# A planner that keeps VectorE's SBUF steps apart from GpSimd's, with new step times and new weights, in a kernel of attention, a mixture of experts and a SoLU layer

## The chip, the cores and the metric

The kernel runs on one core of a Trainium2 chip as one program. The metric is the device time of that program in microseconds (us). The engines are named as in the profile: PE is TensorE's matmul and PEld its weight load, DVE is VectorE, ACT is ScalarE, POOL is GpSimd, SP is SyncE, which here only starts DMAs. In the kernel's own tables GpSimd is called "Pool".

## The reference

Three layers follow one another, all in float32:

```python
# attention: batch 4, heads 12, sequence 448, head size 64
q_n, k_n = rmsnorm(q, g_q), rmsnorm(k, g_k)
scores = q_n @ k_n.T / sqrt(64);  scores -= max(scores, -1)
attn = exp(scores);  attn /= sum(attn, -1) + 1e-9
x = (attn @ v)                    # -> 1792 tokens x 768
# mixture of 8 experts, each token goes to the argmax of x @ w_gate
out[mask] = gate_w * (relu(x[mask] @ w1[e]) @ w2[e])       # 768 -> 1024 -> 768
# SoLU layer: h = x @ w_in; solu = h * softmax(h); layer norm; @ w_out  (768 -> 1024 -> 768)
```

## The kernel before

**Three stages run one after the other.** First attention with the routing of the tokens (about 0 to 323 us of the trace), then the experts, then the SoLU layer with the scattered stores of the output. The change touches the first stage only; the experts and the SoLU layer are written out by hand in a fixed order.

**Attention works on pairs of heads.** There are 24 pairs, in 9 groups of one to three pairs (`GROUPS`). A pair goes through these steps, each a "task" given to the planner with the time it is thought to take:

- *Group steps* (`group`): DMA loads of q, k and v; ScalarE squares q and k (L311, tile `sq`); for some pairs GpSimd adds the two halves of each head's squares (`half`, L315) so that VectorE's sum (L321) reads half as much; then twelve small VectorE steps, the `chain` (L338 to L347), turn the sums into 1/rms (tile `y`). `half=(0, 1, 1)` in the weights says that the second and third pair of each group from the third group on use GpSimd's addition.
- *Norm and turn* (`pair`): GpSimd multiplies q and k by 1/rms (L423, tile `X`, two steps a pair), PE transposes the result into PSUM (L435), ScalarE writes a rounded "high" half (L458, tile `QQ`), VectorE the remainder as "low" (L461, tile `Q`). SP's DMAs then move half tiles between partitions (L468: `QQ<-QQ`, `KS<-Q`, `K<-KS`), so that one product of 128 rows can hold high and low parts.
- *Row maxima*: seven products of 128 queries by 448 keys (L497, tile `r`), each followed by a VectorE maximum (L508, tile `mx`). PE turns the seven maxima (L520), and a DMA puts them into a row of the operand (`Q<-mr`).
- *Scores and exponentials*: seven blocks (`cut` is their order). PE makes the scores (L497, tile `st`), ScalarE the exponentials (L551, tile `pf`), then `part_h` casts them to float16 (L555, tile `ph`) and `part_l` subtracts to get the float16 remainder (L558, tile `pl`).
- *Values*: PE multiplies `ph` and `pl` with the two halves of v (L587 to L589), which ScalarE and VectorE made (L410 and L413, tile `va`), and VectorE divides (L603, L614, L608).
- *Routing*: after each pair PE turns the output and adds to the logits (L728, L739); after each batch of six pairs some twenty VectorE steps (L782 to L860) choose experts and build the token lists (`ohr`, L809, four steps a batch). After the third batch the `order` steps rank the experts by size, and the first six weight tiles of the largest expert are loaded and the first three split (`w_first`, L1109 and L1114). After the fourth batch comes the table of tokens, and GpSimd's gather of the first expert's tokens (L1129, tile `gx`) starts the second stage.

**The order of all this comes from a planner that runs when the program is built** (`Work.run`). It keeps a clock for each engine. In each round it works out, for every task whose inputs are planned, when it could start: when its inputs are done (plus the table `LAT`), when its engine is free, and when the buffer it takes is free (`ring_time`). Of the tasks that could start within `SLACK` of the earliest it takes the one with the smallest weight (`prio`), and emits its instructions. Each engine then executes its instructions in that order on the chip; the planner's times themselves do not exist there, only the order, the choice of buffers, and the choice of engine. A task whose `eng` is a table of several engines goes to the engine on which the planner's clock sees it finish first. `eh` and `el` hold such tables for `part_h` and `part_l` of the seven blocks; `eh2` and `el2` are for the last pair. `PRIO` holds the weights; a task's weight is its pair's number plus the entry.

Before the change the planner treats VectorE and GpSimd as independent engines.

Of the kernel before, what the change touches and what calls it, by code (L numbers as in the profile page):

```python
# [30 lines left out]
class Work:  # L31
# [13 lines left out]
    SEM = 0.0  # L45
    SLACK = 0.02

    def __init__(self, rings):
        self.tasks = []
        self.rings = rings  # L50
        self.users = {}
        self.light = set()
        self.bufs = {}
        self.place = {}
# [4 lines left out]
    def add(self, eng, dur, fn, deps=(), prio=0.0, take=(), use=(), lat=0.0, dma=0.0):  # L59
# [25 lines left out]
    def run(self):  # L85
        T = self.tasks
        n = len(T)
        left = [len(set(t[2])) for t in T]
        after = [[] for _ in T]
        for i, t in enumerate(T):  # L90
            for d in set(t[2]):
                after[d].append(i)
# [5 lines left out]
        count = 0  # L98
        cols = {}

        def ring_time(i):
            at = dict(ready[i])
            for r, key in T[i][4]:
                q = taken[r]
                if len(q) < self.rings[r]:
                    continue
                free_at = None
                for s in q[:1] if r in self.TURN else q:
                    us = self.users[r, s]
                    if any(end[u] is None for u in us):  # L110
                        continue
                    x = max(end[u] for u in us)
                    if free_at is None or x < free_at[0]:
                        free_at = x, us, s
                if free_at is None:
                    return None
                slot[i, r] = free_at[2]
                for u in free_at[1]:
                    for e in at:
                        at[e] = max(at[e], end[u] + self.LAT[eng_of[u]][e] + self.SEM)  # L120
            return at

        slot = {}
        while cand:
            best = []
            for i in cand:
                rt = ring_time(i)
                if rt is None:
                    continue
                es = []  # L130
                for e, d in T[i][0].items():
                    at = max(rt[e], free.get(e, 0.0))
                    es.append((self.pe_end(cols, at, d, i in self.light) if e == "PE" else at + d, at, e))
                fin, start, e = min(es)
                best.append((start, T[i][3], i, fin, e))
            assert best, "no piece of work can start"
            first = min(best)[0]
            start, prio, i, fin, e = min(
                (b for b in best if b[0] <= first + (self.SLACK0 if first < self.START else self.SLACK)), key=lambda b: (b[1], b[0])
            )  # L140
            for r, key in T[i][4]:
                k = len(taken[r])
                if (i, r) in slot:
                    k = self.place[r, slot[i, r]]
                    taken[r].remove(slot[i, r])
                taken[r].append(key)
                self.place[r, key] = k
            T[i][1](e)
            if e == "PE":
                self.pe_end(cols, start, T[i][0][e], i in self.light, True)  # L150
            end[i], eng_of[i], free[e] = fin + T[i][5], e, fin
            if e == "SP" and T[i][6]:

                free["DMA"] = max(fin + 0.65, free.get("DMA", 0.0)) + T[i][6]
                end[i] = free["DMA"] + T[i][5]
            cand.remove(i)
            count += 1
            for j in after[i]:
                for x in ready[j]:
                    ready[j][x] = max(ready[j][x], end[i] + self.LAT[e][x] + self.SEM)  # L160
# [3 lines left out]
        assert count == n  # L164
# [8 lines left out]
class Attention:  # L173
# [103 lines left out]
    def group(self, g, prio):  # L277
# [27 lines left out]
        for j in range(n):  # L305
            for c in cuts:
# [18 lines left out]
                a = add("ACT", 0.02 + 0.117 * w, squares, [l_kq[j]], prio=p, take=[q], use=[kq, gs])  # L325
                if n_ < D:
                    a = add("Pool", 1.12, half, [a], prio=p + 0.2, use=[q])
                reds.append(add("DVE", 0.08 + 0.155 * w * n_ / D, reduce, [a], prio=p + 0.4, use=[q, gs]))


        def chain(cut, nm, d, prio):
# [17 lines left out]
            for f in steps:  # L349
                a = f is first  # L350
                d = [add("DVE", 0.2, f, d, prio=prio, take=[key] if a else (), use=[gs] + [key] * (not a))]
# [25 lines left out]
        d = add("ACT", 0.2 + 0.37 * n, sumsq, l_v, prio=prio + P["vs"], use=[vv, gs])  # L377
# [13 lines left out]
    def pair(self, m, xt, xkey, last):  # L391
# [23 lines left out]
        d = add("ACT", 0.7, v_high, [self.vs], prio=pv, take=[va_], use=[vk, gs])  # L415
        v_done = self.init3 * (m < 3) + [d, add("DVE", 1.0, v_low, [d], prio=pv, use=[va_, vk, gs])]
# [28 lines left out]
        for w in range(2):  # L445
            i = 2 * m + w
            d_n.append(add("Pool", (1.15, 0.88)[w], lambda e, w=w: norm(e, w), [self.rms[j][w], last.get("norm")], prio=i + P["norm"], take=[X] if w == 0 else [], use=[kq, gs] + [X] * w))
# [24 lines left out]
            for rows, to in cuts:  # L472
                d_h.append(add("ACT", 0.56, lambda e, a=rows, b=to, f=high: f(e, a, b), [d, self.G_done] + d_l, prio=i + P["high"], use=[rT, op]))
                d_l.append(add("DVE", 0.63, lambda e, a=rows, b=to, f=low: f(e, a, b), [d_h[-1]], prio=i + P["low"], use=[rT, op]))
# [36 lines left out]
        for s in range(NS):  # L511
# [4 lines left out]
            d_m.append(add("DVE", 0.57, lambda e, s=s: reduce(e, s), [d0], prio=pr, use=[r, mx]))  # L516
# [21 lines left out]
        d = add({"DVE": 0.18, "ACT": 0.2}, 0, copy_max, [d], prio=pr, take=[mr], use=[r])  # L538
# [24 lines left out]
        for k, s in enumerate(P["cut"]):  # L563
# [7 lines left out]
            d = add(eh[s], 0, lambda e, s=s: part_h(e, s), [d, d_pp] + self.init3 * (m < 2), prio=pr + P["ph"], take=a, use=[pf] + u)  # L571
            if k == 0:
                d_pp = d
            d_p[s] = [d, add(el[s], 0, lambda e, s=s: part_l(e, s), [d], prio=pr + P["pl"], use=[pf, pp])]
# [16 lines left out]
        for w in range(2):  # L591
# [21 lines left out]
            d = add("DVE", 0.19, div1, d, prio=pr, take=[den], use=[gs, av])  # L613
            d = add("DVE", 0.16, lambda e, h=h: V.reciprocal(h["den"], h["den"]), [d], prio=pr, use=[den])  # L614
            last["x"] = add("DVE", 0.4, div3, [d, last.get("x")], prio=pr, take=[xkey] if w == 0 else [], use=[den, av] + [xkey] * w)
# [6 lines left out]
        end=1,  # L622
        half=(0, 1, 1),
        cut=(0, 1, 3, 2, 5, 6, 4),
        cutp=(11.35, 2.17, -0.07, 3.29, -13.81, 10.44, 0.89),
        eh=({'ACT': 0.49, 'DVE': 0.55}, {'ACT': 0.49, 'DVE': 0.55}, {'ACT': 0.49}, {'ACT': 0.49}, {'ACT': 0.49}, {'ACT': 0.49}, {'ACT': 0.49}),
        el=({'Pool': 1.13}, {'Pool': 1.13}, {'Pool': 1.13}, {'DVE': 0.8, 'Pool': 1.13}, {'DVE': 0.8, 'Pool': 1.13}, {'Pool': 1.13}, {'Pool': 1.13}),
# [1226 lines left out]
```

## Time and profile before

| | |
|---|---|
| runs shown | 899.03 us median of 3 (896.51 to 904.44) |
| the profiled execution's own time | 896.94 us |
| its span, first to last instruction | 895.2 us |
| PE busy | 811.1 us (91% of the span) |
| PEld busy | 740.8 us (83%) |
| DVE busy | 641.4 us (72%) |
| ACT busy | 497.8 us (56%) |
| POOL busy | 395.1 us (44%) |

The shares are averages over three stages with different limits; the first stage alone is what the change touches. A row of the list by line reads: line, engine, operation, tile written and tiles read, shapes, how often; then the time its instructions cover in us and the mean of one in ns; then the idle time of the engine just before them and what ended it. The profiled execution is 2.1 us under the median of the runs shown.

### The profile page before, as it was taken

How to read it: one execution, taken by the hardware profiler on the slowest of the kernel's cores; microseconds unless marked ns; L12 is line 12 of the kernel's file. 1: busy time of each engine (PE TensorE's matmuls, PEld its weight loads, DVE VectorE, ACT ScalarE, POOL GpSimd, SP SyncE). 2: the span in 40 equal slices, each digit the busy share in tenths (PEclk: the TensorE clock that was granted, in tenths of full speed). 3: DMA queues.
4: the chain of work that ended last, by engine and by line, in shares of the span. 5: the costliest groups of instructions: out<-in, count | busy, mean ns of one | idle time of the engine just before them, and what ended most of it. 6: DMA issues, size and time to landing. Idle time of an engine off the chain costs nothing.

```text
span 895.2 us, 18893 instructions
## 1 busy us (share of the span) xinstructions
PE 811.1 (91%) x6811; PEld 740.8 (83%) x6811; DVE 641.4 (72%) x1484; ACT 497.8 (56%) x958; POOL 395.1 (44%) x420
## 2 busy tenths in 40 slices
PE   2788998987898959989999999899899999999994
PEld 2577887776787849979999999789779989998994
DVE  7988998897898937998667778788575434444541
ACT  7787988886885805644455556667532323332221
POOL 4777898787784624543674125545110000000000
PEclk9999999999997979999999999999999999999998
DMA  7476575574743355757666777767000000000001
GB/s 207 125 200 171 134 197 145 146 197 83 198 111 83 117 118 164 222 187 244 209 220 202 260 229 250 243 211 245 2 1 36 19 36 19 18 18 36 19 18 38
DMA packets 63871, 120.29 MB, mean 134 GB/s; under 512 B 12159, under 2 KB 35290, under 8 KB 63774
## 3 DMA queue, kind: packets, MB, share of 16 engines
q1 hardware_dynamic: 60478, 107.69, 40.8%
q0 software_dynamic: 3296, 11.35, 4.0%
q8 instruction: 56, 0.92, 0.4%
q14 instruction: 41, 0.34, 0.1%
HBM read 86.08 MB, written 11.03 MB: 108 GB/s over the span
## 4 chain that ended last, share of the span: by engine, by line
PE 36%; issue 26%; DVE 17%; DMA 13%; ACT 4%; POOL 2%; SPq 1%; POOLq 0%; ACTq 0%; DVEq 0%
DMA out_dram<-ot,tok 5%; PE st L497 4%; DMA QQ<-QQ 3%; PE h L1157 3%; DVE mx L508 2%; PE h L1158 2%; PE y L1157 2%; PE h L1159 2%; PE y L1158 2%; PE y L1159 2%; PE r L497 2%; PE h L1154 2%; DMA gx<-xd,gx 2%; PE y L1154 2%; DMA rkq<-in_kq_dram 2%
## 5 line engine op out<-in xcount | busy, mean ns | idle before, releaser
L558 POOL TENSOR_TENSOR pl<-pf,ph 128x448 f16<-128x448 f32 x153 | 166.1, 1105 | 47.7 <-ACT ph L555 16.8
L1359 POOL DMA_INDIRECT out_dram<-ot,tok x14 | 13.8, 987 | 214.3 <-ACT ot L1358 208.8
L508 DVE TENSOR_REDUCE mx<-r 128x1 f32<-128x448 f32 x168 | 99.4, 611 | 12.3 <-PE r L497 11.9
L1114 POOL TENSOR_TENSOR wl<-wr,wh 128x768 fp32r<-128x768 f32 x34 | 64.5, 1899 | 93.6 <-ACT wh L1109 93.1
L1109 ACT CAST wh<-wr 128x768 fp32r<-128x768 f32 x128 | 104.7, 831 | 1.6 <-DMA wr<-in_wmoe_dram 1.6
L1114 DVE TENSOR_TENSOR wl<-wr,wh 128x768 fp32r<-128x768 f32 x94 | 97.5, 1037 | 10.5 <-ACT wh L1109 9.0
L551 ACT ACTIVATE pf<-st 128x448 f32<-128x448 f32 x168 | 86.7, 544 | 22.0 <-PE st L497 19.5
L497 PE MATMUL r<-KS,QQ 128*128 128x448 f32 x192 | 69.0, 428 | 21.0 <-DMA QQ<-QQ 12.1
L555 ACT CAST ph<-pf 128x448 f16<-128x448 f32 x153 | 82.5, 569 | 0.3
L587 PEld LDWEIGHTS <-ph 128*128 128x128 f16 x768 | 71.0, 97 | 12.0 <-issue 10.9
L587 PE MATMUL av<-va,ph 128*128 128x65 f16 x768 | 80.1, 194 | 0.0
L588 PE MATMUL av<-va,ph 128*128 128x64 f16 x768 | 79.7, 195 | 0.0
L589 PE MATMUL av<-va,pl 128*128 128x65 f16 x768 | 79.3, 193 | 0.0
L497 PE MATMUL st<-QQ,KS 128*128 128x448 f32 x192 | 74.4, 408 | 2.7 <-ACT pf L551 2.6
L1320 DVE TENSOR_TENSOR cl<-ct,ch 128x512 fp32r<-128x512 f32 x28 | 18.1, 686 | 80.3 <-ACT ch L1319 80.2
L589 PEld LDWEIGHTS <-pl 128*128 128x128 f16 x768 | 71.6, 99 | 0.0
L588 PEld LDWEIGHTS <-ph 128*128 128x128 f16 x768 | 71.4, 97 | 0.1
L497 PE MATMUL st<-Q,K 128*128 128x448 f32 x192 | 68.7, 378 | 0.5 <-DMA K<-KS 0.5
L1154 PE MATMUL y<-hh,wh 128*128 128x384 f32 (+1 forms) x192 | 61.0, 354 | 7.7 <-DVE hh L1203 7.4
L1154 PE MATMUL h<-xx,wh 128*128 128x384 f32 (+1 forms) x192 | 63.0, 364 | 0.4 <-DVE xx L1184 0.4
L497 PEld LDWEIGHTS r<-KS,QQ 128*128 128x128 f32 x192 | 35.5, 199 | 31.1 <-DVE mx L508 5.9
L1157 PE MATMUL h<-xx,wh 128*128 128x280 f32 (+1 forms) x192 | 57.4, 299 | 0.7 <-DVE hh L1203 0.7
(282 smaller groups left out, 2525.9 us busy)
## 6 DMA issues: line engine op xcount, KB each, us to landing
wr<-in_wmoe_dram SPq DMA_DIRECT2D x128, 384.0 KB
rkq<-in_kq_dram SPq DMA_DIRECT2D x24, 448.0 KB
di<-in_w_in_dram SPq DMA_DIRECT2D x16, 384.0 KB
rv<-in_v_dram SPq DMA_DIRECT2D x24, 256.0 KB
do<-in_w_out_dram SPq DMA_DIRECT2D x16, 384.0 KB
K<-KS SPq DMA_DIRECT2D x48, 112.0 KB
KS<-Q SPq DMA_DIRECT2D x48, 112.0 KB
QQ<-QQ SPq DMA_DIRECT2D x48, 112.0 KB
```

The source lines that it names most:

```text
L497: nc.tensor.matmul(ps[:, :S], H[w][x + "x"][:, columns(w, s)], H[w][y], start=(k == 0), stop=(k == len(n) - 1))
L508: V.tensor_reduce(C["mx"][:, s : s + 1], C["sm", s][:, :S], axis=AX.X, op=ALU.max, negate=True)
L551: nc.scalar.activation(C["pf", s], C["st", s][:, :S], AF.Exp)
L555: (eng[e].copy if e == "ACT" else eng[e].tensor_copy)(ph[s][:, :S], C["pf", s])
L558: eng[e].tensor_tensor(pl[s][:, :S], C["pf", s], ph[s][:, :S], op=ALU.subtract)
L587: nc.tensor.matmul(o, hp, vs[:, 0:65], start=(s == ss[0]), stop=False)
L588: nc.tensor.matmul(o[:, 0:64], hp, vs[:, 65:129], start=False, stop=False)
L589: nc.tensor.matmul(o, lp, vs[:, 0:65], start=False, stop=(s == ss[-1]))
L1109: self.nc.scalar.copy(wh, raw)
L1114: (eng or self.nc.vector).tensor_tensor(wl, raw, f32(wh), op=ALU.subtract)
L1154: mm(ps[:, : 2 * n], wh, xx[:, : 2 * n], start=start, stop=False)
L1157: mm(ps[:, :n], wh, xh, start=start, stop=False)
```

## The change

**The model.** A task may now carry `port=True`; such tasks are kept in a set. All GpSimd tasks, and the VectorE tasks with that mark, are kept apart in the planner's clock: a GpSimd task that would start while a marked VectorE task runs is put at that task's end, and the reverse. Marked are the `chain` steps, `v_low` (L413), `part_h` and `part_l` when on VectorE, and those routing steps that read SBUF only. Not marked are steps with an operand in PSUM and the sums and maxima.

**The step times** of the ScalarE, VectorE and GpSimd tasks are new (for example `chain` steps 0.2 to 0.12 us, `v_low` 1.0 to 0.66, `part_h` on VectorE 0.55 to 0.3 and on ScalarE 0.49 to 0.46, `part_l` on VectorE 0.8 to 0.63 and on GpSimd 1.13 to 1.01).

**The weights** are all new, and with them the order of the blocks, the engine tables and `half`, which is now `(0, 0, 0)`: GpSimd's additions (L315) are gone, and VectorE's sums read the whole of the squares. `part_h` may go to VectorE in five of seven blocks (two before; four of the last pair's, two before), `part_l` in two of seven (two before; three of the last pair's, three before).

**Book-keeping.** `self.lg` becomes a table by batch, `ring_time` keeps results it has worked out, and a task that takes two buffers of one ring is handled. What each task computes is the same.

The core of the diff:

```diff
+    def add(self, eng, dur, fn, deps=(), prio=0.0, take=(), use=(), lat=0.0, dma=0.0, port=False):
+        if port:
+            self.port.add(t)
...
+        pool, dve = (0.0, 0.0), (0.0, 0.0)
...
+                for e, d in t[0].items():
+                    x = max(at[e], free.get(e, 0.0))
+                    if e == "Pool" and dve[0] <= x < dve[1]:
+                        x = dve[1]
+                    elif e == "DVE" and i in port and pool[0] <= x < pool[1]:
+                        x = pool[1]
...
+            elif e == "Pool":
+                pool = start, fin
+            elif e == "DVE" and i in port:
+                dve = start, fin
...
-                    a = add("Pool", 1.12, half, [a], prio=p + 0.2, use=[q])
-                reds.append(add("DVE", 0.08 + 0.155 * w * n_ / D, reduce, [a], prio=p + 0.4, use=[q, gs]))
+                    a = add("Pool", 1.1, half, [a], prio=p + 0.2, use=[q])
+                reds.append(add("DVE", 0.02 + 0.14 * w * n_ / D, reduce, [a], prio=p + 0.4, use=[q, gs]))
...
-        norm=57.16, turn=0.15, high=-61.05, low=-14.42, move=-13.07, movek=15.48, max=2.24, mt=-38.68,
-        scores=23.43, exp=-3.7, ph=-3.92, pl=20.82, values=53.83, div=-34.67, kq=-18.37, v=-13.68, sq=-25.7,
-        rms=-120.46, vs=3.07, vprep=6.16, pair=-36.93, route=8.36, order=46.04, first=34.56, soon=2, nv=2,
-        half=(0, 1, 1),
-        cut=(0, 1, 3, 2, 5, 6, 4),
-        eh=({'ACT': 0.49, 'DVE': 0.55}, {'ACT': 0.49, 'DVE': 0.55}, {'ACT': 0.49}, {'ACT': 0.49}, {'ACT': 0.49}, {'ACT': 0.49}, {'ACT': 0.49}),
-        el=({'Pool': 1.13}, {'Pool': 1.13}, {'Pool': 1.13}, {'DVE': 0.8, 'Pool': 1.13}, {'DVE': 0.8, 'Pool': 1.13}, {'Pool': 1.13}, {'Pool': 1.13}),
+        norm=129.16, turn=-60.25, high=-118.25, low=-108.84, move=8.38, movek=31.93, max=-7.33, mt=-37.11,
+        scores=-9.0, exp=-29.71, ph=-45.83, pl=18.65, values=140.45, div=-29.01, kq=-175.45, v=-3.02,
+        sq=-21.28, rms=-143.95, vs=79.27, vprep=-13.14, pair=-59.93, route=27.67, order=183.91, first=81.87,
+        half=(0, 0, 0),
+        cut=(3, 2, 4, 0, 1, 5, 6),
+        eh=({'ACT': 0.46, 'DVE': 0.3}, {'ACT': 0.46}, {'ACT': 0.46}, {'ACT': 0.46, 'DVE': 0.3}, {'ACT': 0.46, 'DVE': 0.3}, {'ACT': 0.46, 'DVE': 0.3}, {'ACT': 0.46, 'DVE': 0.3}),
+        el=({'Pool': 1.01}, {'Pool': 1.01}, {'Pool': 1.01}, {'Pool': 1.01}, {'DVE': 0.63, 'Pool': 1.01}, {'Pool': 1.01}, {'DVE': 0.63, 'Pool': 1.01}),
```

## Rows read from the trace of the kernel before

**Rows 1.** Three stretches: us, busy us (instructions) of each engine, granted PE clock, DMA share, GB/s.

```profile
0.00:25.00 25.00, 7.84 (x29) 6.28 (x29) 18.96 (x75) 18.37 (x33) 11.12 (x93) 1.00 0.64 187
25.00:325.00 300.00, 267.75 (x3451) 232.02 (x3452) 263.66 (x651) 234.47 (x471) 222.37 (x211) 0.96 0.55 145
325.00:895.00 570.00, 535.53 (x3333) 502.53 (x3332) 358.80 (x759) 244.94 (x456) 161.60 (x118) 0.98 0.40 127
```

**Rows 2.** Waits of PE from 25 to 325 us: us in total, times, longest.

```profile
PE r L497 <- DMA QQ<-QQ: 8.4, 6, 2.3
PE r L497 <- DMA Q<-mr: 3.4, 1, 3.4
PE r L435 <- POOL X L423: 3.1, 1, 3.1
```

**Rows 3.** The chain that ended last, 25 to 325 us, shares by line (cut by the view).

```profile
by line: PE st L497 12.3%; DMA QQ<-QQ 8.6%; DVE mx L508 7.4%; PE r L497 6.7%; issue 6.0%; PE av L587 3.7%; PE av L588 3.6%; PE av L589 3.6%; PE r L435 3.0%; DVE Q L461 3.0%; PE r L739 2.7%; DVE ohr L809 2.6%; DMA KS<-QQ 2.5%; DVE y L347 2.2
```

**Rows 4.** Single lines: shortest/median/longest in ns, first and last start, shapes.

```profile
L558 POOL TENSOR_TENSOR pl<-pf,ph x153: 1028/1042/1747, 30.6 to 312.2; 128x448 f16<-128x448 f32 x153
L558 DVE TENSOR_TENSOR pl<-pf,ph x15: 608/1100/1465, 48.0 to 309.7; 128x448 f16<-128x448 f32 x15
L413 DVE SCALAR_TENSOR_TENSOR va<-rv,ve,va x24: 734/982/1477, 23.2 to 300.5; 128x512 f16<-128x512 f32 x24
L555 DVE CAST ph<-pf x15: 356/382/1108, 44.3 to 310.6; 128x448 f16<-128x448 f32 x15
L345 DVE TENSOR_TENSOR u<-y x30: 158/194/1047, 7.9 to 249.0; 128x42 f32<-128x42 f32 x21, 128x8 f32<-128x8 f32 x3, 128x6 f32<-128x6 f32 x3, 128x28 f32<-128x28 f32 x3
L346 DVE TENSOR_TENSOR u<-u,ms x30: 160/188/1046, 8.1 to 249.7; 128x42 f32<-128x42 f32 x21, 128x8 f32<-128x8 f32 x3, 128x6 f32<-128x6 f32 x3, 128x28 f32<-128x28 f32 x3
L347 DVE SCALAR_TENSOR_TENSOR y<-u,y x30: 160/192/950, 8.3 to 250.4; 128x42 f32<-128x42 f32 x21, 128x8 f32<-128x8 f32 x3, 128x6 f32<-128x6 f32 x3, 128x28 f32<-128x28 f32 x3
L809 DVE TENSOR_SCALAR ohr<-cols,rk x16: 291/316/1132, 130.3 to 322.2; 112x384 f16<-112x384 f16 x16
L461 DVE SCALAR_TENSOR_TENSOR Q<-r,G,QQ x48: 662/674/691, 16.2 to 278.6; 128x448 fp32r<-128x448 f32 x46, 64x448 fp32r<-64x448 f32 x2
```

**Rows 5.** List by line, 0 to 520 us: count, then busy us, mean ns, idle before.

```profile
L345 DVE TENSOR_TENSOR u<-y 128x42 f32<-128x42 f32 x21 | 9.6, 456 | 0.0
L346 DVE TENSOR_TENSOR u<-u,ms 128x42 f32<-128x42 f32 x21 | 8.7, 414 | 0.0
L347 DVE SCALAR_TENSOR_TENSOR y<-u,y 128x42 f32<-128x42 f32 x21 | 9.4, 446 | 0.0
L809 DVE TENSOR_SCALAR ohr<-cols,rk 112x384 f16<-112x384 f16 x16 | 9.6, 627 | 0.0
L558 DVE TENSOR_TENSOR pl<-pf,ph 128x448 f16<-128x448 f32 x15 | 15.8, 1051 | 0.3 <-ACT ph L555 0.2
L555 ACT CAST ph<-pf 128x448 f16<-128x448 f32 x153 | 82.5, 569 | 0.3
L555 DVE CAST ph<-pf 128x448 f16<-128x448 f32 x15 | 7.7, 516 | 0.2 <-ACT pf L551 0.2
L315 POOL TENSOR_TENSOR sq<-sq 128x448 f32<-128x448 f32 x14 | 15.9, 1135 | 11.3 <-ACT sq L311 11.3
L321 DVE TENSOR_REDUCE ms<-sq 128x14 f32<-128x896 f32 x9 | 9.7, 1078 | 2.1 <-ACT sq L311 2.1
L321 DVE TENSOR_REDUCE ms<-sq 128x14 f32<-128x448 f32 x14 | 8.4, 603 | 1.5 <-POOL sq L315 1.5
```

**Rows 6.** The chain that ended last, 150 to 200 us, shares by line (cut by the view).

```profile
by line: issue 15.2%; DMA QQ<-QQ 10.1%; POOL sq L315 9.1%; DMA rkq<-in_kq_dram 8.9%; DVE mx L508 7.0%; PE st L497 5.1%; ACT pf L551 4.1%; DVE x L608 3.0%; ACT sq L311 2.8%; DVE Q L461 2.6%; DVE ms L321 2.5%; ACT ph L555 2.5%; PE r L497 2.3%
```

**Rows 7.** The same chain, 318 to 340 us, in order of time: start us, us, what.

```profile
320.33 0.34 DVE tkp L803
...
325.58 9.60 DMA gx<-xd,gx
```

**Rows 8.** ScalarE's split of expert weights, 270 to 345 us: columns as in Rows 4.

```profile
L1109 ACT CAST wh<-wr x6: 818/840/846, 306.5 to 343.5; 128x768 fp32r<-128x768 f32 x6
```

More of the change, by code (lines that the diff above doesn't have):

```diff
@@ L52, in __init__ @@
         self.light = set()
+        self.port = set()
+        self.last = 0.0
         self.bufs = {}
@@ L87, in run @@
         n = len(T)
-        left = [len(set(t[2])) for t in T]
+        deps = [set(t[2]) for t in T]
+        left = [len(d) for d in deps]
         after = [[] for _ in T]
-        for i, t in enumerate(T):
-            for d in set(t[2]):
-                after[d].append(i)
+        for i, d in enumerate(deps):
+            for x in d:
+                after[x].append(i)
         ready = [dict.fromkeys(t[0], 0.0) for t in T]
@@ L97, in run @@
         cand = [i for i in range(n) if left[i] == 0]
-        count = 0
-        cols = {}
+        cols, light, port, LAT = {}, self.light, self.port, self.LAT
+        users, rings, place = self.users, self.rings, self.place
+        todo = {k: len(v) for k, v in users.items()}
+        held = [[] for _ in T]
+        for k, v in users.items():
+            for u in v:
+                held[u].append(k)
+        done = {}
+        slot = {}
+        pool, dve = (0.0, 0.0), (0.0, 0.0)
         def ring_time(i):
@@ L102, in ring_time @@
             at = dict(ready[i])
+            new, chosen = {}, set()
             for r, key in T[i][4]:
                 q = taken[r]
-                if len(q) < self.rings[r]:
+                new[r] = new.get(r, 0) + 1
+                if len(q) + new[r] <= rings[r]:
                     continue
-                free_at = None
+                best = None
                 for s in q[:1] if r in self.TURN else q:
-                    us = self.users[r, s]
-                    if any(end[u] is None for u in us):
+                    if todo[r, s] or (r, s) in chosen:
@@ L111, in ring_time @@
                         continue
[L112 to L115, printed above, removed]
-                    return None
-                slot[i, r] = free_at[2]
-                for u in free_at[1]:
+                    x = done.get((r, s))
+                    if x is None:
+                        x = done[r, s] = max(end[u] for u in users[r, s])
+                    if best is None or x < best[0]:
+                        best = x, s
@@ L125, in run @@
+            return at
+        for _ in range(n):
             best = []
             for i in cand:
-                rt = ring_time(i)
-                if rt is None:
+                t = T[i]
+                at = ring_time(i) if t[4] else ready[i]
+                if at is None:
                     continue
[L130 to L133, printed above, removed]
@@ L136, in run @@
+                best.append((b[1], t[3], i, b[0], b[2]))
             assert best, "no piece of work can start"
             first = min(best)[0]
[L138 to L141, printed above, removed]
+            first += self.SLACK0 if first < self.START else self.SLACK
+            start, prio, i, fin, e = min((b for b in best if b[0] <= first), key=lambda b: (b[1], b[0]))
@@ L149, in run @@
+            t[1](e)
             if e == "PE":
[L150 to L155, printed above, removed]
+                self.pe_end(cols, start, t[0][e], i in light, True)
+            elif e == "Pool":
+                pool = start, fin
+            elif e == "DVE" and i in port:
+                dve = start, fin
@@ L156, in run @@
+            end[i], eng_of[i], free[e] = fin + t[5], e, fin
+            if e == "SP" and t[6]:
+                free["DMA"] = max(fin + 0.65, free.get("DMA", 0.0)) + t[6]
+                end[i] = free["DMA"] + t[5]
+            self.last = max(self.last, fin) if e == "PE" else self.last
+            for k in held[i]:
+                todo[k] -= 1
             cand.remove(i)
-            count += 1
             for j in after[i]:
-                for x in ready[j]:
-                    ready[j][x] = max(ready[j][x], end[i] + self.LAT[e][x] + self.SEM)
+                rj = ready[j]
+                for x in rj:
+                    y = end[i] + LAT[e][x]
+                    if y > rj[x]:
+                        rj[x] = y
@@ L446, in pair @@
             i = 2 * m + w
-            d_n.append(add("Pool", (1.15, 0.88)[w], lambda e, w=w: norm(e, w), [self.rms[j][w], last.get("norm")], prio=i + P["norm"], take=[X] if w == 0 else [], use=[kq, gs] + [X] * w))
+            d_n.append(add("Pool", (1.02, 0.81)[w], lambda e, w=w: norm(e, w), [self.rms[j][w], last.get("norm")], prio=i + P["norm"], take=[X] if w == 0 else [], use=[kq, gs] + [X] * w))
             last["norm"] = d_n[-1]
```

103 lines of the change are left out of this document (55 added, 48 removed).

## Prediction

> **What bounds the kernel now.** I started with busy time by stretch. The code that is written by hand holds the last 570 us and isn't touched; PE is busy there for 535.53 us [rows 1], so all that the change can win or lose lies before 325 us. In the first 25 us PE works only 7.84 us [rows 1], since nothing is there to multiply yet; the change can't do much about that. From 25 to 325 us no engine is full: PE is busy 267.75 of 300 us, VectorE 263.66, ScalarE 234.47, GpSimd 222.37 [rows 1]. The reader should see that PE and VectorE are level and both near nine tenths: the stage is held by the order in which several nearly full in-order queues meet. PE's idle time there, 300 − 267.75 = 32 us, is about what a better order can return.
>
> Next, what PE waits for: the moves of QQ end 8.4 us of it, the move of the maxima 3.4, GpSimd's norm 3.1 [rows 2]. Each of these follows VectorE or GpSimd steps: the move of QQ needs L461, the maxima need L508, the norm needs the twelve `chain` steps. Then the chain of waits, which tells what the time passes through: beside PE's products it holds VectorE's maxima (7.4%), its lows (3.0%), the token lists (2.6%) and the last step of `chain` (2.2%) [rows 3].
>
> Last, the spread of single lines. It shows the loss that the new model is about. VectorE steps with all operands in SBUF vary by a factor of two to six: the remainder takes 608 to 1465 ns, the low half of v 734 to 1477, the cast 356 to 1108, a 42-column `chain` step about 190 to 1047, the lists 291 to 1132 [rows 4]. The step that reads PSUM, L461, has the same width and stays within 662 to 691. What the first have too much is below one GpSimd step, 1042 ns [rows 4], as if they wait for a running GpSimd step to end; the planner has them run freely.
>
> **The change part by part.** *Collisions on the path.* In `chain` the excess of the mean over the median (mostly free) step is 456 − 194, 414 − 188 and 446 − 192 ns, or 57%, 55% and 57% of the means [rows 4, 5]. L347 stands on the chain of waits with 2.2% of 300 us, 6.6 us; L345 and L346 run with it, one of each for one, at like means, and I estimate the same 6.6 us for each: 19.8 us on the path, and 56% of it, 11.1 us, is waiting. The lists stand there with 2.6%, 7.8 us, and (627 − 316) / 627 = 50% of that is excess [rows 3 to 5]: 3.9 us. Together 15 us. Bounds: nothing, if the new order collides elsewhere; and from above also the excess that lies beside the path, 15 × (1051 − 608) ns = 6.6 us of remainders and 24 × (982 − 734) ns = 6 us of v, so 28 us. I take 15, since only those rows are seen on the path. What is late next is PE: of its 32 us of idle time about half would be left, the start of each group and the moves behind L461 above all.
>
> *GpSimd's additions go.* 14 steps of 1135 ns leave GpSimd (15.9 us) and 14 sums on VectorE grow from 603 to 1078 ns, 6.65 us more [rows 5]. On the path, between 150 and 200 us, L315 has 9.1% of 50, 4.55 us or four steps [rows 6]; four sums grow by 4 × 0.475 = 1.9 us. Net 2.6 us won. Elsewhere neither is seen on the path: the sum runs beside PE's products of other pairs. If that cover goes, the other ten sums cost 4.75 us; from the other side, ten GpSimd steps of queueing are gone, 11 us, so −5 to +11 around it.
>
> *Casts move to VectorE.* Places where `part_h` may choose grow from 48 to 119 of 168 (23 pairs × 5 + 4). Before, 15 of the 48 went to VectorE [rows 5]. At that rate 37 would go, 22 more; the bounds are 0 and 104 more. Each takes 569 ns from ScalarE and puts 516 ns on VectorE with today's collisions, 356 without [rows 4, 5]. For 22 that is 8 to 11 us on VectorE and 12.5 off ScalarE. Both have more room than that (36.3 and 65.5 us [rows 1]), so I count zero; the cover is VectorE's idle time, and what it costs when gone is the last rival. `part_l` may choose in 49 places as before, and is also zero.
>
> *Weights of moves, loads, turns, maxima.* They set the order in the queues of SP, PE and the others; no row prices an order that isn't there. Between −12 us (PE's waits for the moves of QQ and of the maxima, 8.4 and 3.4 us [rows 2], all gone) and +12 for as much again, I take zero: nothing in the rows leans to a side. The granted clock of the stretch is 0.96 [rows 1]; I leave it there.
>
> *The hand-over.* `order` and `first` get larger weights, so the ranking of the experts and the first six weight loads come later among ready steps. They can't come too late for the ranking itself, which L803 at 320.33 us reads. The first weight cast stands at 306.5 us [rows 8], and the gather of the first tokens runs 9.60 us from 325.58 [rows 7] before PE needs weights: that hides a load and a cast of 0.84 us. But six loads on SP's queue that slide behind 320 us would share the DMA engines with that gather: between nothing and its whole 9.60 us again. Most loads should still land before, so I take a quarter, 2.4 us lost.
>
> *Sum.* −15 − 2.6 + 2.4 = −15.2 us. Against the profiled execution's 896.94 us this is 882 us. That execution is 2.1 us below the median of the runs shown, 899.03, so an after that is measured like them may stand up to 2 us higher.
>
> **Rivals.** *The path is held elsewhere, no change.* The stage is a circle from norm to moves to maxima to scores; the moves of QQ alone hold 8.6% of 300 us, 26 us, of the chain [rows 3], and no step of the change shortens a move. If the time won on `chain` is waited off at the next move, the gain is the 2.6 us of the additions less the 2.4 of the hand-over: 897, with the median's offset 899. For it: DMA is second on the chain. Against it: each move itself follows L461 in VectorE's queue, where the collisions sit.
>
> *GpSimd pays.* GpSimd's remainders also spread, 1028 to 1747 ns [rows 4]: it waits for VectorE's steps as well. Then 22 more casts hold it 22 × 0.356 = 7.8 us. With GpSimd's remainders ahead of the values on PE, this comes back on the path, and the gain is 15 − 8 = 7 us: 890, and at 40 casts nothing. The Trainium skill's page "SBUF — State Buffer", section "SBUF: two separate sides", states it as an exclusive lock: of a VectorE step in a two-port mode (or with two SBUF inputs) and a GpSimd step the first one holds the shared pair for its whole instruction. The trace agrees as far as the longest waits above go (1465 − 608 = 857 ns, below a GpSimd step of 1042). Against this rival: GpSimd loses 15.9 us of additions, and its busy time is the smallest of the four.
>
> *VectorE becomes the bound, slower.* VectorE has 36.3 us left in the stage [rows 1]. The sums take 6.65; casts at 516 ns fill the rest at (36.3 − 6.65) / 0.516 = 57 more. From there each costs its full time: at 80 more, 6.65 + 41.3 − 36.3 = 12 us, 909; at all 104, 24 us, 921. For it: the table's 0.3 us for VectorE against 0.46 for ScalarE invites the choice. Against it: the new model makes a cast wait for GpSimd, so VectorE often finishes later in the planner's clock; and fewer collisions give VectorE room.
>
> *The model doesn't match the chip.* If what spreads the steps isn't GpSimd, the order is only a different one, and I give it to the case of no change.
>
> **How the numbers follow.** About 1% (9 us: below 890 or above 908) is what a measurement of this kernel can tell from no change. The forecast has 0.62: its range is 866 (28 us of collisions and 2.6) to 890. No change has 0.26, of which GpSimd pays 0.11 and the held path 0.15: 890 to 902, the upper end being no gain, the hand-over's 2.4 us lost and the median's offset. VectorE as the bound has 0.12, 909 and up. The range for 8 in 10 is 866 to 902; it leaves out the last case and some 0.05 below. So faster 0.62, same 0.26, slower 0.12.
>
> **What would show it.** Right: L345 to L347 at means near 190 to 250 ns, L809 near 320, the GpSimd remainders' longest near 1042; no L315 and 23 long sums; PE's idle time in the stage down by about half; the last L809 near 307 us instead of 322.2 [rows 4], and everything behind it shifted as one piece. Wrong: VectorE busy above 95% of the stage with over 70 casts on L555; a gather longer than 9.60 us; the same means as before in `chain`; or a stage that shrinks while the later ones grow.

## The result, and the profile after

The changed kernel takes 889.55 us (median of 8 runs, 884.38 to 895.36) against 899.18 us for the kernel before, measured beside it: a ratio of 0.988, with a 95% interval of 0.984 to 0.992. The profiled execution has a span of 885.1 us, 10.1 us less than before, and stands in the lower half of its runs as the one before does. Medians and ratios here and below leave out the few executions that took over 1.5% more than the fastest of their kernel.

Three stretches of the changed kernel; columns as in [rows 1]:

```profile
0.00:25.00 25.00, 8.26 (x32) 6.68 (x32) 18.69 (x73) 19.86 (x35) 11.23 (x93) 1.00 0.71 210
25.00:325.00 300.00, 265.57 (x3454) 229.36 (x3455) 267.70 (x694) 216.31 (x425) 211.46 (x201) 0.94 0.56 145
325.00:895.00 570.00, 531.94 (x3328) 499.11 (x3327) 358.57 (x759) 245.11 (x456) 159.48 (x114) 0.99 0.38 125
```

These windows no longer cut at the same place of the program, so I use two marks: the VectorE step that ends the routing lists (tile `gx`, L828 before, L864 after) and the first expert product. Before, then after, from the order in time (start, us, engine, line):

```profile
323.00 0.18 DVE L828 SCALAR_TENSOR_TENSOR gx<-r,lists 128x24 int32<-128x24 f32 x1 [0.50 <-PE r L873]
...
336.50 0.69 PE L1154 MATMUL h<-xx,wh 128*128 128x384 f32 x1 [0.39 <-DVE xx L1184]
```

```profile
309.91 0.18 DVE L864 SCALAR_TENSOR_TENSOR gx<-r,lists 128x24 int32<-128x24 f32 x1 [0.50 <-PE r L909]
...
327.81 0.44 PE L1190 MATMUL h<-xx,wh 128*128 128x384 f32 x1 [0.61 <-issue]
```

The reader should see three numbers. The attention stage ends 13.1 us earlier. The hand-over from it to the experts takes 17.9 us instead of 13.5, so 4.4 us are given back. From there to the end it is 557.3 us instead of 558.7, the other 1.4 us. Together −13.1 + 4.4 − 1.4 = −10.1.

PE's work up to the end of the lists, before and after; columns as in [rows 1]:

```profile
25.00:323.00 298.00, 266.20 (x3443) 230.46 (x3443) 262.99 (x648) 234.47 (x471) 221.45 (x210) 0.96 0.55 146
```

```profile
25.00:310.00 285.00, 262.95 (x3441) 226.75 (x3441) 264.23 (x688) 213.82 (x422) 207.45 (x197) 0.97 0.54 142
```

PE's idle time falls from 31.8 to about 22 us; the other 3 us of the 13.1 are busy time of the same products.

What PE waits for from 25 to 325 us; columns as in [rows 2]:

```profile
PE r L1022 <- DVE pl_gf L1020: 12.5, 1, 12.5
...
PE r L531 <- DMA QQ<-QQ: 1.7, 2, 1.3
...
PE st L531 <- DMA Q<-mr: 1.4, 2, 1.2
```

The waits for the moves of QQ and of the maxima fell from 8.4 and 3.4 us [rows 2] to 1.7 and 1.4. The 12.5 us at the top are new and belong to the hand-over. The single VectorE and GpSimd lines, shortest/median/longest as in [rows 4], and the list by line as in [rows 5]:

```profile
L592 POOL TENSOR_TENSOR pl<-pf,ph x155: 1026/1042/1783, 36.7 to 297.7; 128x448 f16<-128x448 f32 x155
L447 DVE SCALAR_TENSOR_TENSOR va<-rv,ve,va x24: 714/746/1565, 17.8 to 286.8; 128x512 f16<-128x512 f32 x24
L589 DVE CAST ph<-pf x47: 376/385/1283, 38.8 to 296.2; 128x448 f16<-128x448 f32 x47
L845 DVE TENSOR_SCALAR ohr<-cols,rk x16: 288/312/1100, 260.5 to 309.1; 112x384 f16<-112x384 f16 x16
```

```profile
L379 DVE TENSOR_TENSOR u<-y 128x42 f32<-128x42 f32 x21 | 6.0, 288 | 0.0
L380 DVE TENSOR_TENSOR u<-u,ms 128x42 f32<-128x42 f32 x21 | 5.8, 278 | 0.0
L381 DVE SCALAR_TENSOR_TENSOR y<-u,y 128x42 f32<-128x42 f32 x21 | 4.9, 234 | 0.0
L845 DVE TENSOR_SCALAR ohr<-cols,rk 112x384 f16<-112x384 f16 x16 | 7.1, 475 | 0.0
L589 DVE CAST ph<-pf 128x448 f16<-128x448 f32 x47 | 27.6, 591 | 1.3 <-ACT pf L585 1.2
L355 DVE TENSOR_REDUCE ms<-sq 128x14 f32<-128x896 f32 x23 | 24.7, 1074 | 2.9 <-ACT sq L345 2.9
```

`chain` (now L379 to L381) collides less: means of 288, 278 and 234 ns instead of 456, 414 and 446. But it still does (longest 922 to 1068), and 47 casts that went to VectorE now carry the excess: 47 × (591 − 385) ns = 9.7 us. L315 is gone, and there are 23 long sums.

### The profile page after: what moved, and what is told of

Same layout as the page of the kernel before. It is cut to its first block, busy times and chain, and to the rows that moved or that the text cites. A ratio compares the mean times of both kernels' runs of the same rounds, so it can differ in the third digit from the quotient of the medians.

```text
span 885.1 us, 18862 instructions
## 1 busy us (share of the span) xinstructions
PE 805.8 (91%) x6811; PEld 735.1 (83%) x6811; DVE 645.0 (73%) x1524; ACT 481.3 (54%) x916; POOL 382.2 (43%) x408
## 4 chain that ended last, share of the span: by engine, by line
PE 37%; issue 26%; DVE 19%; DMA 11%; ACT 4%; POOL 1%; SPq 1%; another core or an unknown queue 1%; POOLq 0%; ACTq 0%; DVEq 0%
PE st L531 5%; DMA out_dram<-ot,tok 5%; DVE mx L542 3%; PE r L531 3%; PE h L1193 3%; PE h L1194 2%; PE h L1195 2%; PE y L1193 2%; PE y L1194 2%; PE y L1195 2%; PE h L1190 2%; DMA wr<-in_wmoe_dram 2%; PE y L1190 2%; DVE Q L495 2%; DVE va L447 1%
## 5 line engine op out<-in xcount | busy, mean ns | idle before, releaser
L592 POOL TENSOR_TENSOR pl<-pf,ph 128x448 f16<-128x448 f32 x155 | 169.0, 1112 | 48.7 <-ACT ph L589 17.0
L531 PE MATMUL r<-KS,QQ 128*128 128x448 f32 x192 | 63.6, 416 | 14.4 <-DMA QQ<-QQ 4.2
L589 ACT CAST ph<-pf 128x448 f16<-128x448 f32 x121 | 66.1, 574 | 0.5
L1190 PE MATMUL h<-xx,wh 128*128 128x384 f32 (+1 forms) x192 | 61.0, 355 | 0.6 <-issue 0.6
L457 POOL TENSOR_TENSOR X<-rkq,y 128x512 f32<-128x512 f32 (+1 forms) x48 | 45.8, 966 | 30.1 <-PE r L531 9.7
```

Source lines behind the costliest of these rows:

```text
L531: nc.tensor.matmul(ps[:, :S], H[w][x + "x"][:, columns(w, s)], H[w][y], start=(k == 0), stop=(k == len(n) - 1))
L589: (eng[e].copy if e == "ACT" else eng[e].tensor_copy)(ph[s][:, :S], C["pf", s])
L592: eng[e].tensor_tensor(pl[s][:, :S], C["pf", s], ph[s][:, :S], op=ALU.subtract)
L1190: mm(ps[:, : 2 * n], wh, xx[:, : 2 * n], start=start, stop=False)
```

## The experiments

The labels e1 to e12 are in the order in which they ran. "The lists" means the `gx` step.

### The model and the weights, one without the other

**e1**, the changed kernel without the separation:

```diff
-        if port:
-            self.port.add(t)
...
-                    if e == "Pool" and dve[0] <= x < dve[1]:
+                    if False and dve[0] <= x < dve[1]:
```

> The changed kernel, but the planner no longer keeps marked VectorE steps and GpSimd steps apart; new step times and new weights stay. Theory A (the separation is what shortens the attention stage): collisions return, the 42-column chain steps go back from means of 230 to 290 ns towards 414 to 456, the step that ends the routing lists (309.9 us in the changed kernel, 323.0 before) comes at 318 us or later, and the time is 895 us or more. Theory B (the new weights alone, or less work on GpSimd, do it): that step stays within 3 us of 310 and the time within 5 us of 889. A shift of the order that favours neither would also lengthen the stage, since the weights were fitted to the model with the separation, so the collisions' size decides, not the time alone.

Measured: 920.5 us, ratio 1.026 (1.022 to 1.030); the lists end at 345.5 us. The 42-column steps have means of 347, 448 and 361 ns. From 25 to 345 us, columns as in [rows 1], and the casts:

```profile
25.00:345.00 320.00, 273.51 (x3431) 228.81 (x3429) 307.19 (x750) 200.32 (x379) 203.93 (x182) 0.97 0.49 133
```

```profile
L587 DVE CAST ph<-pf x92: 353/383/1227, 36.3 to 331.7; 128x448 f16<-128x448 f32 x92
```

Time and lists are as theory A says; theory B falls. VectorE has 92 casts (47 in the changed kernel) and 28 remainders (13), and is busy 307 of 320 us, 96%. This is the picture of my rival "VectorE becomes the bound", in a kernel whose planner doesn't know of the collisions. Whether the casts alone make it slow is what e12 asked.

**e2**, the new model and step times with the old `PRIO` (tables of engines at the new times), and **e3**, the old model and step times with the new `PRIO`:

> The kernel with the new model (separation and new step times) but all of the old weights, the old order of blocks, GpSimd's additions and the old choice of engines. Theory A: the model alone gives half or more of what the stage won, the lists end at 311 to 317 us, the time is 887 to 893 us, and the hand-over to the experts stays at its 13.5 us of before. Theory B: with the old weights the stage ends within 3 us of 323 and the time is that of the kernel before, 897 to 899 us.

> The kernel with the old model and old step times but all of the new weights, order of blocks, choice of engines, and no additions on GpSimd. Theory A: without the separation the new weights give nothing, the lists end at 323 us or later and the time is 897 us or more; the weights belong to the model they were found with. Theory B: the stage ends within 3 us of 310 and the time within 5 us of 889.

Measured: e2 907.57 us, ratio 1.011 (1.007 to 1.015), lists at 335.4 us. e3 929.54 us, ratio 1.036 (1.032 to 1.040), lists at 359.7 us. For e3 theory A holds, though its profile shows too much: that execution took 936.86 us, the longest of its five, with a mean granted clock of 0.91 of the full 2.4 GHz from 25 us to the lists (0.97 in the changed kernel). For e2 both theories fail: the model with the old weights doesn't win half and doesn't leave the time as it was, it loses 1%. Its `chain` collides less than before (means 393, 321 and 282 ns), and yet the stage is 12 us longer. PE's waits in e2, 25 to 323 us:

```profile
PE r L531 <- DMA QQ<-QQ: 15.9, 12, 3.7
PE st L531 <- ACT pf L585: 6.0, 6, 4.8
```

So fewer collisions on one chain of steps are no gain by themselves; PE waits longer for the moves of QQ here (8.4 us before [rows 2]).

**e12**, e1 with casts allowed on VectorE only where the kernel before allowed them (`eh` in blocks 0 and 1, `eh2` in 3 and 4):

> As e1 (no separation of VectorE and GpSimd in the planner, new times and weights), but casts may go to VectorE only in the blocks of the kernel before; that makes 43 of them, where e1 had 92 and the changed kernel 47. In e1 VectorE was busy 307 of the 320 us from 25 to 345. Theory E (without the separation the planner sees VectorE as free and gives it so many casts that it becomes the bound; this made e1 slow): VectorE is busy less than 92% of the stage, the lists end at 315 to 328 us instead of 345, and the time is 893 to 906 us. Rival (the colliding order itself makes e1 slow): the lists end at 335 us or later, 912 us or more.

Measured: 916.03 us, ratio 1.016 (1.011 to 1.020), 43 casts, lists at 342.8 us, VectorE 291.29 of 317 us, 92%. Theory E falls as far as the casts go: half of them are gone and the lists end only 2.7 us earlier. But VectorE isn't much relieved, since 37 remainders went to it now, so a VectorE with too much work isn't excluded as the reason for both. An order that was planned without the separation is slow with many casts and with few. What e1 to e3 and e12 can't tell, beside that, is how much of that is the separation and how much that the weights were fitted to a model that has it, since every edit to the planner gives another order.

### The same order with one thing taken away

The next five leave the planner as it is; only what an instruction does, or which engine does it, differs.

**e5**, for theory C, the moves behind the bulk loads:

```diff
-            nc.sync.dma_start(t["kq"][:, j], self.kq[b, p0 + j])
+            if g < 4:
+                nc.sync.dma_start(t["kq"][:, j], self.kq[b, p0 + j])
+            else:
+                nc.sync.dma_start(t["kq"][:, j, 0, 0], self.kq[b, p0 + j, :, 0, 0])
```

(v in the same way, which makes 15 of the 24 loads of each small; the two buffers of each are allocated once.)

> The kernel before with its order unchanged; from the fifth group on each bulk load of q, k and v brings only a slice of 256 bytes a partition (the rest of the tile keeps older heads' data, so the output and the routing differ, and only the attention stage is compared: the step that ends the routing lists, 323.0 us before). It is there because the kernel with the new model and old weights had fewer collisions than before and yet a longer stage, with PE waiting 15.9 us for the moves of QQ (8.4 before, 1.7 in the changed kernel), and because the longest moves (6.6 and 7.1 us on the chain) were issued right behind bulk loads on SP's queue. Theory C (moves that queue behind bulk loads set the stage before): PE's wait for QQ falls under 3 us and the lists end 8 us or more earlier, at 315 or less. Theory A (collisions of VectorE and GpSimd set it): within 4 us of 323.

Measured: the lists end at 322.84 us, 0.2 us from the kernel before, and PE still waits 5.7 us for QQ (its total time holds other work, since the routing differs). Theory C falls for these loads: they don't set the stage. This is one execution.

**e6**, the kernel before with GpSimd's remainders cut to 32 columns, and **e9**, the same edit in the changed kernel:

```diff
-            eng[e].tensor_tensor(pl[s][:, :S], C["pf", s], ph[s][:, :S], op=ALU.subtract)
+            n = 32 if e == "Pool" else S
+            eng[e].tensor_tensor(pl[s][:, :n], C["pf", s][:, :n], ph[s][:, :n], op=ALU.subtract)
```

> The kernel before with its order unchanged; GpSimd's remainder steps subtract only 32 of the 448 columns (the other remainders are zero, which leaves their part of the values out). GpSimd's long steps, with which VectorE collides most, are gone. Theory A: the chain steps fall to means under 300 ns, and the lists end 12 us or more before 323.0 us, at 311 or less, the time 885 us or less. Theory C: VectorE's steps get short all the same but PE waits for the moves of QQ as before (8 us), and the lists end within 5 us of 323.

> The changed kernel with its order unchanged; GpSimd's remainder steps subtract only 32 of 448 columns (the rest of those remainders is zero, a part of the values that is left out), as was done to the kernel before, where it ended the lists 11.0 us earlier and made the time 0.992 of before. Theory A (the new order wins by avoiding collisions on the path): little is left to win, the lists end within 4 us of 309.9, the time is 886 us or more. Theory D (the collisions cost the changed kernel as much as before, and its gain comes from the order of the other steps, ScalarE's relief and the additions that went): the lists end 8 us or more earlier, the time is 882 us or less.

Lists by line in e6 and in e9, columns as in [rows 5]:

```profile
L561 POOL TENSOR_TENSOR pl<-pf,ph 128x32 f16<-128x32 f32 x153 | 42.3, 281 | 154.5 <-ACT ph L557 57.1 <-issue 56.3 <-POOL pl L561 7.9
...
L812 DVE TENSOR_SCALAR ohr<-cols,rk 112x384 f16<-112x384 f16 x16 | 4.6, 311 | 0.0
L347 DVE TENSOR_TENSOR u<-y 128x42 f32<-128x42 f32 x21 | 4.3, 207 | 0.0
L348 DVE TENSOR_TENSOR u<-u,ms 128x42 f32<-128x42 f32 x21 | 4.1, 196 | 0.0
L349 DVE SCALAR_TENSOR_TENSOR y<-u,y 128x42 f32<-128x42 f32 x21 | 4.1, 193 | 0.0
```

```profile
L591 DVE CAST ph<-pf 128x448 f16<-128x448 f32 x47 | 19.6, 420 | 3.1 <-ACT pf L587 2.8
```

With GpSimd's long steps gone, the same VectorE instructions in the same order fall to 207, 196 and 193 ns (456, 414 and 446 before) and the lists to 311 ns (627). That settles what spreads them [rows 4]. The price in the kernel before: the lists end at 312.02 us, 11.0 us earlier, and the time is 890.07 us, ratio 0.992 (0.989 to 0.995), which is 7 us. The profiled execution of e6 took 885.57 us, 4.5 us less than the median of its runs, so the 11.0 us may be too much. Theory A asked for 12 us and 885 us, a little more than came; theory C falls, since the lists moved by more than 5 us and PE's wait for QQ fell to 3.8 us. In the changed kernel the lists end at 304.33 us, 5.6 us earlier; 885.06 us, ratio 0.987 (0.984 to 0.991), which the runs can't tell from the changed kernel's 0.988. So the new order still pays, by the profiles, about half of what the old one paid; by the times, what it still pays isn't shown to differ from nothing. Neither theory A (within 4 us) nor theory D (8 us or more) has the lists. Both runs leave out a part of the values and make GpSimd itself quicker, and GpSimd's other long steps stay, so 11.0 and 5.6 us are estimates for the collisions alone.

**e11**, the 47 casts at their place in the program, but on ScalarE:

```diff
-            (eng[e].copy if e == "ACT" else eng[e].tensor_copy)(ph[s][:, :S], C["pf", s])
+            nc.scalar.copy(ph[s][:, :S], C["pf", s])
```

> The changed kernel with its order unchanged, but the 47 casts that the planner gave to VectorE are executed by ScalarE at the same place in the program. I counted the move of casts as zero: then the time stays within 4 us of 889 us, VectorE's 28 us of casts going against 27 us more on ScalarE. Theory D's share for the casts (ScalarE's relief is part of the gain): ScalarE gets near 90% of the stage, its exponentials come late for PE, and the time is 895 us or more.

Measured: 892.02 us, ratio 0.991 (0.988 to 0.995); the lists end at 313.76 us, 3.9 us later than in the changed kernel. PE's largest wait from 25 to 325 us is now for the exponentials (0.3 us in the changed kernel):

```profile
PE st L531 <- ACT pf L585: 6.1, 10, 1.9
```

By time this lies inside "within 4 us", so "zero" isn't refuted. ScalarE is busy 235.65 of 300 us, 79%, and not near 90%, and the time stays under theory D's 895 us. What the profile shows is a wait that the casts on VectorE take from PE, as theory D names it; that they won the 3.9 us isn't shown, since the lists of e4 below, with the same order, end 3.2 us later than in the changed kernel too.

**e10**, GpSimd's remainder as two instructions of 224 columns:

```diff
-            eng[e].tensor_tensor(pl[s][:, :S], C["pf", s], ph[s][:, :S], op=ALU.subtract)
+            for c in (slice(0, S // 2), slice(S // 2, S)) if e == "Pool" else (slice(0, S),):
+                eng[e].tensor_tensor(pl[s][:, c], C["pf", s][:, c], ph[s][:, c], op=ALU.subtract)
```

> The changed kernel with its order unchanged; each of GpSimd's remainder steps is two instructions of 224 columns, nothing is left out. If a VectorE step waits for the end of the running GpSimd instruction, the longest waits halve, from about 850 ns to about 400, at the price of one more instruction's fixed time on GpSimd, which has idle time (211 of 300 us busy). Theory D: half of what the collisions cost comes back, 3 to 6 us, 884 to 886 us. Theory A, or GpSimd's longer steps eat it: 888 to 892 us.

Measured: 888.24 us, ratio 0.990 (0.987 to 0.992), lists at 311.13 us: no gain. GpSimd's two halves take 2 × 664 ns, and VectorE's remainders didn't get shorter (mean 1103 ns against 991). GpSimd is busy 237.92 us from 25 to 325 us instead of 211.46, so that its longer steps eat the gain, as the expectation has it, stays possible beside the long waits that the last section shows; no run separates the two.

### The hand-over

The chain that ended last in the changed kernel, 302 to 330 us, in order of time (start us, us, what):

```profile
308.22 12.11 DMA wr<-in_wmoe_dram
320.35 0.84 ACT wh L1145
321.21 0.96 DVE wl L1150
...
322.39 0.39 PE r L1022
322.77 2.99 PE r L1537 x16
```

The third weight load, issued behind two others and ahead of the gather, lands 12 us later. VectorE's third split waits for it, the table's copy waits behind that split in VectorE's queue, and PE's turn and its warm-up products wait for the copy: this is the wait of 12.5 us above. Before, the first split stood at 306.5 us [rows 8], before the lists were done.

**e4** takes the third split out of the planned stage:

```diff
-            if k >= 3:
+            if k >= 2:
                 raws[key] = t
...
         plan.use(wk)
+        w_high()
+        w_low()
```

> The changed kernel with one step moved: the third split of expert weights leaves the planner's stage and is issued after the transposes of the first tokens. In the changed kernel VectorE's third split waits for a load until 321.2 us, and the copy of the table, PE's turn of it and the warm-up products wait behind it in VectorE's and PE's queues, while 17.9 us pass from the end of the lists to the first expert product (13.5 before). Theory A (that wait in VectorE's queue makes the hand-over long): the first product comes 3 to 5 us earlier, 884 to 887 us. Rival (the gather shares the DMA engines with six weight loads and lands late anyway): the first product moves by less than 1 us and the time stays at 888 to 890 us.

Measured: 888.18 us, ratio 0.991 (0.988 to 0.994). In its profile the hand-over is 14.4 us (313.09 to 327.51), 3.5 less, as theory A says; but the lists ended 3.2 us later in that execution, with the same order of the attention steps, and the time moved by 1.4 us, inside the spread of the runs. By time the rival's number holds. The 3.2 us also tell how far one execution's stage is from another's.

**e7** and **e8** change only three weights of the changed kernel (e7: `route=8.36, order=46.04, first=34.56`; e8: `route=-98.24, order=-50.19, first=66.45`):

> The changed kernel with the three weights of the routing, the ranking and the first weight loads put back (route 8.36, order 46.04, first 34.56); all else as changed. In the changed kernel all routing is left to the end, the loads are issued at 307.1 and 309.6 us, and 17.9 us pass from the end of the lists to the first expert product. Theory A of the hand-over (the weight loads meet the gather): the loads are issued before 300 us, the hand-over is back at 13 to 14.5 us, and with a stage within 3 us of the changed kernel's the time is 884 to 888 us. Rival (the stage lengthens by what the hand-over wins, since the routing steps then sit among the last pairs): 888 to 892 us.

> The changed kernel with the routing steps pulled forward (route -98.24, order -50.19, first 66.45): each batch's routing runs as soon as its logits are there, as in the kernel before, and the weight loads come some 20 us before the end of the stage. Theory A of the hand-over: 13 to 14.5 us from the lists to the first product, and 884 to 888 us. Rival: routing steps among the pairs take VectorE's time and collide with GpSimd, the stage is 3 us or more longer than the changed kernel's, and the time is 888 us or more.

Measured: e7 896.9 us, ratio 1.000 (0.997 to 1.004); e8 901.3 us, ratio 1.001 (0.998 to 1.004). In the profiles the hand-over is back at 13.4 us (313.92 to 327.30) and 13.9 us (324.59 to 338.52). In e8 the stage paid for it, as its rival says: the lists end at 324.59 us, so there leaving the routing to the end is worth more in the stage than it costs in the hand-over. In e7 they end at 313.92 in the profile, but that execution took 889.96 us, the fastest of all its runs, so it shows less than the usual loss, and where the rest of that loss sits isn't shown. The time of e7 fits neither of its expectations, 884 to 888 us and 888 to 892. None of the twelve is shown to beat the changed kernel.

## Why the prediction was right, point by point

The sign, the place and the range were right: faster by 9.6 us (15 forecast), in the attention stage, with the rest shifted as a piece. But 889.55 us lies 0.45 us inside the upper end of "faster", and 890 was also the number of the rival "GpSimd pays", so that the range held is in part luck. The terms came out otherwise than they were sized; the stage's numbers are from single profiles, good to about 3 us.

- **Collisions on the path, −15.** The mechanism is shown by e6: the excess of [rows 4, 5] goes when GpSimd's long steps go. The size was too large. All of it cost the kernel before about 11.0 us, and the new order still pays about 5.6, so by this estimate from four single profiles it regained 5.4. The step that failed is "I take 15": I took the excess of four rows off the path as if nothing would come in their place. The chain that ended last in the changed kernel, 25 to 310 us, shares by line (cut by the view):

```profile
by line: PE st L531 15.1%; DVE mx L542 10.0%; PE r L531 8.6%; issue 4.9%; DVE va L447 4.3%; DMA wr<-in_wmoe_dram 4.2%; PE av L621 4.1%; PE av L622 4.0%; PE av L623 4.0%; DVE Q L495 3.9%; DMA KS<-QQ 3.5%; PE r L775 3.0%; PE r L469 2.8%; DVE 
```

  Added up over all pieces of this chain and of the one before, from 25 us to the end of the lists, the three last `chain` steps and the lists (`ohr`) hold 10.6 us instead of 26.6. But VectorE's low halves of v, its casts and its remainders hold 25.0 us instead of 6.3: the collisions went partly to the casts, which I had priced at 356 to 516 ns and counted as zero, and which have a mean of 591. What the path lost is the moves of QQ, 6.5 us instead of 25.9.
- **GpSimd's additions, −2.6.** L315 is gone and 23 sums take 1074 ns, as said. The effect alone wasn't tried, so its size isn't shown.
- **Casts, 0.** 47 went to VectorE where I estimated 37. By e11 they won 3.9 us in the profile and 2.5 us in the median, neither clear of the noise.
- **Order of the other weights, 0 (−12 to +12).** PE's waits for QQ and the maxima fell from 11.8 to 3.1 us. How much of this is the order and how much fewer collisions isn't shown: what is left of the 13.1 us, 13.1 − 5.4 − 3.9 = 3.8 us for this and the additions, is no larger than the error of the numbers that it is taken from. No run changes the weights of the moves, loads, turns and maxima alone.
- **The hand-over, +2.4.** It was 4.4. I had the place right (weight loads that meet the gather) and missed who waits behind: VectorE's third split holds the table's copy, and that holds PE. The remark that most loads should still land before was wrong; three were issued at 307 us and three from 309.6 us on. And the term has only the price of leaving the ranking and the loads to the end: e7, which puts these two weights and the routing's back, has the time of the kernel before, so together they gain more than they cost.
- **The rivals.** "The path is held elsewhere" fell with the waits for QQ, "GpSimd pays" too: its remainders have the same median of 1042 ns, and a mean of 1112 ns against 1105. "VectorE becomes the bound" isn't the changed kernel, but it is e1. The end of the lists at 309.9 us against my "near 307" for the last L809 (309.1 now) was close.
- **The signs that did not come.** The lists have a mean of 475 ns and not about 320, two of the three `chain` steps 278 and 288 and not up to 250, and GpSimd's longest remainder 1783 and not about 1042: the new order collides less, not hardly at all. PE's idle time in the stage fell by a third and not by half.

What stays open: the model and its weights don't add up. Each alone makes the kernel slower (1.011 and 1.036), together they make it 1.2% faster, and the runs can't separate a better model from weights that fit it.

## What to carry to other kernels

When instructions of the same shape take between one and six times the shortest, look which engine runs during the long ones, and price them by a run that keeps the order and shortens the other engine's steps (e6): the sum of the excess on the chain was too much here, 15 us forecast against about 11 by that run and about 5 regained, since other steps took their place on the path. Here neither the planner's new weights nor its new model won anything without the other; test them as a pair. After a stage gets shorter, follow who waits behind each late load in every in-order queue, up to the next stage's first product.

## What the runs showed of the hardware that I had not expected

A VectorE step doesn't always get in at the end of the GpSimd instruction that it meets. In e10, one remainder of VectorE took 4.30 us, where the shortest takes 614 ns. GpSimd first, then VectorE, from 179.9 to 184.4 us (start, us, engine, line):

```profile
179.37 1.18 POOL L593 TENSOR_TENSOR pl<-pf,ph 128x224 f16<-128x224 f32 x2
180.51 1.05 POOL L457 TENSOR_TENSOR X<-rkq,y 128x512 f32<-128x512 f32 x1
181.51 2.31 POOL L593 TENSOR_TENSOR pl<-pf,ph 128x224 f16<-128x224 f32 x4
```

```profile
180.00 4.30 DVE L593 TENSOR_TENSOR pl<-pf,ph 128x448 f16<-128x448 f32 x1
184.23 0.74 DVE L447 SCALAR_TENSOR_TENSOR va<-rv,ve,va 128x512 f16<-128x512 f32 x1
```

The VectorE step starts at 180.00. In its time six GpSimd instructions (the second of the first row, the one of the second, the four of the third) follow each other without a gap until 183.82, and it ends 0.48 us after the last of them. It waited for a pause of GpSimd, not for one instruction. So cutting GpSimd's step in two doesn't bound the waits. Three lines of e10, columns as in [rows 4]:

```profile
L846 DVE TENSOR_SCALAR ohr<-cols,rk x16: 289/313/753, 262.9 to 310.3; 112x384 f16<-112x384 f16 x16
L589 DVE CAST ph<-pf x47: 360/389/2450, 40.2 to 296.7; 128x448 f16<-128x448 f32 x47
L593 DVE TENSOR_TENSOR pl<-pf,ph x13: 614/900/4301, 43.3 to 295.7; 128x448 f16<-128x448 f32 x13
```

The longest of the lists fell to 753 ns from 1100 in the changed kernel, but the longest cast rose to 2450 ns from 1283 and the longest remainder to 4301 ns from 1491. The Trainium skill's page "SBUF — State Buffer", section "SBUF: two separate sides", says that of a VectorE step with two SBUF inputs and a GpSimd step the first one holds the shared pair for the whole instruction; the trace agrees with that, and shows in this place that further GpSimd instructions may run ahead of a VectorE step that waits. In the kernel before and in the changed one no remainder waited longer than one GpSimd step: the longest take 1465 and 1491 ns.

The same program's runs also spread more than 1%: 884.38 to 895.36 us for the changed kernel. In e4, whose attention steps have the same order, the stage ended 3.2 us later, so one profile's stage is good to about 3 us; what makes the executions differ isn't shown.
